# Float16 hi/lo operands for the second layer of a block attention + feed-forward kernel, from the third token group on

## The chip, the cores and the metric

The kernel runs on one core of one Trainium2 chip. The metric is the device time of one execution in microseconds (us); shorter is better. Three runs of the kernel before took 890.31, 891.81 and 893.53 us, median 891.81 us. Engines are named as in the profile: PE is the matrix engine, PEld its weight loads, DVE the vector engine, ACT the scalar engine, POOL the GpSimd engine, SP the engine that issues the DMAs.

## The reference

Attention over independent blocks of 64 positions, for 8 batches and 8 heads of dimension 64, gives 4608 tokens of 512 numbers. A feed-forward part follows, with w_in of 512x2048 and w_out of 2048x512, all in float32:

```python
scores = scale * np.matmul(q_c, k_c.transpose(0, 1, 2, 4, 3))
attn = softmax(scores)
x = np.matmul(attn, v_c)          # 4608 x 512
h = x @ w_in
g = h - np.tanh(h)
return g @ w_out
```

q and k are drawn with a spread of about 0.43, v with 0.1. The result is wanted at close to float32 accuracy, so the kernel splits each operand of a product into a high and a low part and makes three products, hi*hi, hi*lo and lo*hi.

## The kernel before

The 4608 tokens are nine groups of 512 (four tiles of 128). For each group the feed-forward part runs over 16 units; a unit (fc) is a slice of 128 of the 2048 hidden numbers. `FeedForward.gemm1` (L413) makes a unit's hidden slice `ph` in PSUM with 12 matmuls of 512 columns, whose operands are float16 hi/lo pairs (`wih`, `wil`, `xh`, `xl`). `shrink` makes g of it: ACT takes the tanh (L421), DVE makes h - tanh(h) into `t` (L422), ACT rounds it to the high part `gh` (L425), DVE subtracts to get the low part `gl` (L426). Here gh and gl are float32r tiles, and so are the parts `woh`, `wol` of w_out. `gemm2` (L434) then makes 12 matmuls of 512 columns, three (gh*woh, gh*wol, gl*woh) for each of the group's four token tiles, and adds them into four PSUM tiles `po` that gather over all 16 units. gemm2 of a unit is issued two units after its gemm1 (`LAG = 2`), so a group starts with three gemm1 in a row and ends with two gemm2 in a row. `ph`, gh and gl have two buffers each. After the 16 units `finish` copies `po` to SBUF, two tiles by ACT (L459) and two by DVE (L457), and SP writes them out.

Between the units of a group the attention of the next group is worked (`interleaved`), one pair of blocks after another: `split` makes float16 hi/lo parts of q, k, v (ACT L307, L310, L316; DVE L308, L311, L317), `scores` (PE L325), `softmax`, `transpose` by DMA, `values` (PE L359). Since float16 has a narrow range, q, k and v of a group are first multiplied by a power of two. `Late.sums` finds it: `spread` (ACT L96) sums |a| * 2^-12 over 2048 numbers of each partition, once each for q, k and v; POOL takes the maximum over partitions (`power`, L103), and DVE makes the power and its inverse.

The first group is different: in it the weights come in (as bits of 64-bit numbers), are converted, and split; w_in to float16 with a power of its own for each pair of units, w_out to float32r.

What sets the order: the code names, for each half step of a group, what is emitted there (a table `at`; key 2s is after gemm1 of unit s, 2s+1 after the gemm2 that follows). For the first steps PE and SP have an order written out by hand; behind that the framework's scheduler sets each engine's order, and may move an instruction of ACT, DVE or POOL well ahead of where the code names it. On the chip each engine takes its instructions in the order that was built.

## Time and profile before

The profiled execution took 890.42 us, and its span (first to last instruction) is 888.3 us.

| | us |
|---|---|
| median of three runs | 891.81 |
| profiled execution, its span | 890.42, 888.3 |
| first group, until the second starts | 154.25 |
| second group | 91.76 |
| third to eighth group, each | 91.76 |
| ninth group, until its last matmul starts | 85.6 |
| PE busy over the span | 866.5 (98%) |
| DVE busy | 538.5 (61%) |
| ACT busy | 471.3 (53%) |
| POOL busy | 15.5 (2%) |
| mean granted PE clock, share of full | 0.989 |

A line of a group of instructions reads: source line, engine, operation, tile written <- tiles read, shapes, count | busy us in all, mean ns of one | idle us of the engine before them, and what ended that. A line of a timeline reads: start, duration, engine, line, operation, tiles, count, and in brackets the idle time ahead of it and what ended it. Matmuls overlap: one of 512 columns is listed with some 390 ns, and the next starts some 220 ns after it, so the distance of starts is what counts.

### The profile page before, as it was taken

The numbers are of one execution on the slowest core, as the hardware profiler recorded it, in microseconds if no ns is written. First come the engines' busy times: TensorE is split into PE (matmuls) and PEld (weight loads), VectorE is DVE, ScalarE is ACT, GpSimd is POOL, SyncE is SP. The second block draws the span as 40 slices with busy tenths as digits, with TensorE's granted clock in tenths as the row PEclk, the third lists the DMA queues.
The fourth block names the chain that finished last, engine by engine and source line by source line (L and its number), as shares of the span: only waits on it lengthen the run. The fifth ranks groups of instructions, "written<-read, shape, count | busy, mean of one in ns | idle before, by whom it ended". The sixth has DMA issues, their size and how long they took to land.

```text
span 888.3 us, 13109 instructions
## 1 busy us (share of the span) xinstructions
PE 866.5 (98%) x5163; PEld 566.8 (64%) x5163; DVE 538.5 (61%) x976; ACT 471.3 (53%) x824; POOL 15.5 (2%) x32
## 2 busy tenths in 40 slices
PE   7999898999999999999999999999999999999997
PEld 4786655566656666666666666666666666665665
DVE  6798896667666665656466745674567456533222
ACT  8589773756646544555455634663366344423221
POOL 0000003000000000000000000000000000000000
PEclk8899999999999999999999999999999999999999
DMA  9584333312221121212112211132111100010001
GB/s 261 184 233 133 136 122 121 117 36 66 78 83 51 34 72 61 61 47 72 60 53 53 74 60 37 49 89 66 37 48 24 60 13 13 13 54 6 1 1 48
DMA packets 61373, 62.71 MB, mean 71 GB/s; under 512 B 32640, under 2 KB 40832, under 8 KB 61312
## 3 DMA queue, kind: packets, MB, share of 16 engines
q1 hardware_dynamic: 61312, 61.88, 23.8%
q8 instruction: 40, 0.66, 0.3%
q14 instruction: 21, 0.17, 0.1%
HBM read 45.09 MB, written 9.44 MB: 61 GB/s over the span
## 4 chain that ended last, share of the span: by engine, by line
PE 91%; ACT 4%; issue 2%; DVE 2%; DMA 0%; POOL 0%; ACTq 0%; DVEq 0%; POOLq 0%
PE po L434 42%; PE ph L413 40%; PE psa L359 2%; PE psa L325 2%; PE psa L258 2%; PE psa L210 1%; ACT junk L96 1%; ACT s L228 1%; PE ph L501 1%; ACT wih L152 0%; ACT w_out L126 0%; ACT s L241 0%; DVE w_out L127 0%; PE psa L160 0%; ACT w_in L126 0%
## 5 line engine op out<-in xcount | busy, mean ns | idle before, releaser
L434 PE MATMUL po<-woh,gh 128*128 128x512 f32 x576 | 245.6, 426 | 3.3 <-ACT gh L425 3.3
L434 PE MATMUL po<-wol,gh 128*128 128x512 f32 x576 | 225.9, 392 | 0.0
L434 PE MATMUL po<-woh,gl 128*128 128x512 f32 x576 | 225.8, 394 | 0.0
L422 DVE SCALAR_TENSOR_TENSOR t<-ph,sig,t 128x512 f32<-128x512 f32 (+1 forms) x148 | 108.7, 734 | 146.7 <-ACT t L421 146.5
L413 PEld LDWEIGHTS <-wih 128*128 128x128 f16 x1184 | 106.4, 98 | 137.4 <-issue 25.7
L421 ACT ACTIVATE t<-ph,sig 128x512 f32<-128x512 f32 (+1 forms) x148 | 99.8, 674 | 168.0 <-PE ph L413 167.7
L426 DVE TENSOR_TENSOR gl<-t,gh 128x512 fp32r<-128x512 f32 (+1 forms) x148 | 99.8, 675 | 111.4 <-ACT gh L425 111.2
L413 PE MATMUL ph<-xh,wih 128*128 128x512 f16 (+1 forms) x592 | 150.8, 377 | 5.5 <-ACT wih L152 5.5
L425 ACT CAST gh<-t 128x512 fp32r<-128x512 f32 (+1 forms) x148 | 89.4, 604 | 126.0 <-PE po L434 101.5
L413 PE MATMUL ph<-xh,wil 128*128 128x512 f16 (+1 forms) x592 | 149.3, 375 | 0.2 <-DVE wil L153 0.2
L413 PE MATMUL ph<-xl,wih 128*128 128x512 f16 (+1 forms) x592 | 148.5, 373 | 0.0
L434 PEld LDWEIGHTS po<-woh,gh 128*128 128x128 f32 x576 | 108.5, 188 | 34.4 <-ACT gh L425 5.7
L434 PEld LDWEIGHTS po<-woh,gl 128*128 128x128 f32 x576 | 108.0, 188 | 24.5 <-DVE gl L426 0.5
L434 PEld LDWEIGHTS po<-wol,gh 128*128 128x128 f32 x576 | 108.5, 188 | 21.5
L413 PEld LDWEIGHTS <-wil 128*128 128x128 f16 x592 | 58.0, 98 | 67.3 <-issue 1.1
L317 DVE SCALAR_TENSOR_TENSOR v16l<-rawv,to,v16h 64x512 f16<-64x512 f32 x56 | 41.8, 746 | 5.6 <-ACT v16h L316 4.7
L316 ACT ACTIVATE v16h<-rawv,to 64x512 f16<-64x512 f32 x56 | 40.1, 716 | 6.0 <-PE psa L359 4.5
L307 ACT ACTIVATE q16h<-rawq,to 64x512 f16<-64x512 f32 x56 | 40.3, 720 | 4.3 <-DVE exp L297 3.2
L308 DVE SCALAR_TENSOR_TENSOR q16l<-rawq,to,q16h 64x512 f16<-64x512 f32 x56 | 41.6, 744 | 1.3
L345 ACT CAST a<-s 128x512 f16<-128x512 f32 x28 | 17.3, 616 | 30.7 <-DVE s L339 27.9
L333 ACT ACTIVATE s<-s,exp 128x512 f32<-128x512 f32 x28 | 20.1, 719 | 17.2 <-DVE s L332 17.1
L457 DVE COPY t<-po 128x512 f32<-128x512 f32 x18 | 12.4, 690 | 26.8 <-PE po L434 14.3
(98 smaller groups left out, 760.2 us busy)
## 6 DMA issues: line engine op xcount, KB each, us to landing
out<-t SPq DMA_DIRECT2D x36, 256.0 KB, 2.1
raw_in<-w_in SPq DMA_DIRECT2D x16, 512.0 KB, 5.3
raw_out<-w_out SPq DMA_DIRECT2D x16, 512.0 KB, 3.8
rawq<-qL SPq DMA_DIRECT2D x28, 256.0 KB, 2.6
rawk<-kL SPq DMA_DIRECT2D x28, 256.0 KB, 3.0
rawv<-vL SPq DMA_DIRECT2D x28, 256.0 KB, 2.6
qbd<-qE SPq DMA_DIRECT2D x16, 128.0 KB, 4.4
k<-kE SPq DMA_DIRECT2D x8, 256.0 KB, 4.5
```

The costliest lines, as they stand in the source:

```text
L258: nc.tensor.matmul(ps[:, hp, cs], lhsT=d["v"][:, hp, :, c], rhs=d["aT"][:, hp, cs], start=True, stop=True)
L307: nc.scalar.activation(qh[r, :, r], q[r], AF.Copy, scale=to[r, 0:1])
L308: nc.vector.scalar_tensor_tensor(out=ql[r, :, r], in0=q[r], scalar=to[r, 0:1], in1=qh[r, :, r], op0=ALU.mult, op1=ALU.subtract)
L316: nc.scalar.activation(vh[r, :, r], v[r], AF.Copy, scale=to[r, 2:3])
L317: nc.vector.scalar_tensor_tensor(out=vl[r, :, r], in0=v[r], scalar=to[r, 2:3], in1=vh[r, :, r], op0=ALU.mult, op1=ALU.subtract)
L333: nc.scalar.activation(s, s, AF.Exp, scale=d["exp"])
L413: nc.tensor.matmul(ph, lhsT=wi[fc // 2][a][:, fc % 2, kc * P:(kc + 1) * P], rhs=x[b][:, kc, cols], start=(k == 0), stop=(k == 3 * KC - 1))
L421: nc.scalar.activation(t, ph, AF.Tanh, scale=sig)
L422: nc.vector.scalar_tensor_tensor(out=t, in0=ph, scalar=sig, in1=t, op0=ALU.mult, op1=ALU.subtract)
L425: nc.scalar.copy(out=gh, in_=t)
L426: nc.vector.tensor_sub(gl, t, gh)
L434: nc.tensor.matmul(self.po[t], lhsT=gg[a][:, ts], rhs=wo[fc][b], start=(fc == 0 and i == 0), stop=(fc == FC - 1 and i == 2))
```

## The change

From the third group on, gemm2's operands are float16 pairs in place of float32r pairs. Three things make that possible.

* A power of two for w_out (one for all of it), and one for g in each group. That of g comes from a bound: x is a weighted mean of values v, so |x| is at most the largest |v|, and |h| at most that times the sum over a column of |w_in|; `Half.power_of` takes the power of v of this group, a power for w_in and a factor 2^-20. For this bound `Late.sums` now takes v's largest |v| on DVE (`largest`, a TENSOR_REDUCE) where ACT summed |v| before. The inverse is applied when `po` is copied out.
* The maxima of the weights. Over the second group's steps, ACT sums |woh| of each of the 16 units (`spread`, 128x512, and the reading of its sum), DVE takes the largest |wih| of each of 8 pairs of units (128x1024), then `powers` takes the maximum of both over the partitions on POOL (`htop`).
* The conversion, in the second half of the second group. For each unit `convert` adds woh and wol into a float32 tile `whole` on POOL (two buffers), ACT writes the high float16 part and DVE the low one into a new tile of the same name and place as woh (one buffer, so it takes the place of the float32r part once the second group's gemm2 of that unit is done). The second group itself still uses float32r.

In `shrink` ACT's rounding becomes an activation with a scale (gh) and DVE's subtraction a scalar_tensor_tensor (gl), both to float16.

```diff
+    def largest(a, out):
+        nc.vector.tensor_reduce(out=out, in_=a, axis=AX.X, op=ALU.max, apply_absolute_value=True)
+        nc.vector.tensor_scalar_mul(out, out, 2.0 ** -12)
...
             some = self.raw[n][:, :SIZES[g]]
-            spread(self.pool, some, d["sums"][:, "qkv".index(n):"qkv".index(n) + 1])
             if n != "v":
+                spread(self.pool, some, d["sums"][:, "qkv".index(n):"qkv".index(n) + 1])
                 return
+            largest(some.rearrange("p i n -> p (i n)"), d["sums"][:, 2:3])
...
+    class Half:
+        def __init__(self, pool):
...
+        def steps(self):
+            at = defaultdict(list)
+            for fc in range(FC):
+                at[fc + 3].append(lambda fc=fc: spread(self.pool, wo[fc][0].bitcast(F32), self.parts[:, fc:fc + 1]))
+                if fc % 2:
+                    at[fc + 3].append(lambda j=fc // 2: largest(wi[j][0].rearrange("p a n -> p (a n)"), self.w_in[:, j:j + 1]))
+                at[max(FC + 4 + fc, 2 * fc + 2 * LAG + 1)].append(lambda fc=fc: self.convert(fc))
+            at[FC + 3].append(self.powers)
+            return at
+        def powers(self):
+            both = self.pool.tile([P, 2], F32, name="both")
+            nc.vector.tensor_mul(self.w_in, self.w_in, from_w)
+            nc.vector.reduce_max(out=both[:, 0:1], in_=self.w_in, axis=AX.X)
+            nc.vector.reduce_max(out=both[:, 1:2], in_=self.parts, axis=AX.X)
+            power(self.pool, "h", both, self.to, self.back)
+        def convert(self, fc):
+            w = self.pool.tile([P, DM], F32, name="whole", bufs=2)
+            nc.gpsimd.tensor_add(w, wo[fc][0].bitcast(F32), wo[fc][1].bitcast(F32))
+            half = wo_pool[fc].tile([P, DM], F32R, name=f"woh{fc}").bitcast(F16).rearrange("p (a n) -> p a n", a=2)
+            h, l = self.wo[fc] = half[:, 0], half[:, 1]
+            to = self.to[:, 1:2]
+            nc.scalar.activation(h, w, AF.Copy, scale=to)
+            nc.vector.scalar_tensor_tensor(out=l, in0=w, scalar=to, in1=h, op0=ALU.mult, op1=ALU.subtract)
+        def power_of(self, g):
+            to, undo = (const.tile([P, 1], F32, name=n, bufs=2) for n in ("to_g", "undo_g"))
+            nc.vector.scalar_tensor_tensor(out=to, in0=to_x[g], scalar=2.0 ** -20, in1=self.to[:, 0:1], op0=ALU.mult, op1=ALU.mult)
...
@@ shrink
-            gh = ffn.tile([P, MOST], F32R, name="gh")[:, :n]
-            gl = ffn.tile([P, MOST], F32R, name="gl")[:, :n]
-            nc.scalar.copy(out=gh, in_=t)
-            nc.vector.tensor_sub(gl, t, gh)
+            if self.undo_g is not None:
+                gh, gl = (ffn.tile([P, MOST], F32R, name=f"g{a}").bitcast(F16)[:, :n] for a in "hl")
+                nc.scalar.activation(gh, t, AF.Copy, scale=self.to_g)
+                nc.vector.scalar_tensor_tensor(out=gl, in0=t, scalar=self.to_g, in1=gh, op0=ALU.mult, op1=ALU.subtract)
+            else:
...
@@ gemm2
-                    nc.tensor.matmul(self.po[t], lhsT=gg[a][:, ts], rhs=wo[fc][b], start=..., stop=...)
+                    nc.tensor.matmul(self.po[t], lhsT=gg[a][:, ts], rhs=self.wo[fc][b], start=..., stop=...)
...
     for g in range(1, NG):
-        ff = FeedForward(g, x)
+        ff = FeedForward(g, x, half if g > 1 else None)
...
+        at = interleaved(att, g + 1, nx) if nx else {}
+        if g == 1:
+            for k, fs in half.steps().items():
+                at[k] += fs
```

How the built order moves, at three places. The first is ACT from the last unit of the first group to the first units of the second. Before, the two copies of `po` are followed by one sum of |q|, and then the second group's first tanh (`t<-ph,sig`):

```order
L425 CAST gh<-t 128x512
L459 COPY t<-po_104 128x512
L459 COPY t<-po_545 128x512
L96 ACTIVATE junk_1731,sums<-rawq 128x2048
L421 ACTIVATE t<-ph,sig 128x512
L96 ACTIVATE junk_1753,sums<-rawk 128x2048
L425 CAST gh<-t 128x512
L421 ACTIVATE t<-ph,sig 128x512
L96 ACTIVATE junk_1767,sums<-rawv 128x2048
```

Now (`sums_out` are the sums of |woh|):

```order
L490 CAST gh<-t 128x512
L99 ACTIVATE junk_1868,sums_out<-woh_92 128x512
L99 ACTIVATE junk_1909,sums_out<-woh_1091 128x512
L99 ACTIVATE junk_1942,sums_out<-woh_1094 128x512
L99 ACTIVATE junk_1974,sums_out<-woh_1097 128x512
L529 COPY t<-po_104 128x512
L529 COPY t<-po_545 128x512
L99 ACTIVATE junk_1741,sums<-rawq 128x2048
L99 ACTIVATE junk_1999,sums_out<-woh_1100 128x512
L99 ACTIVATE junk_1765,sums<-rawk 128x2048
L481 ACTIVATE t<-ph,sig 128x512 x2
```

Eleven of the 16 sums of |woh| have moved into the first group's tail, the seven before these rows among them, and the first tanh of the second group now stands behind the sum of |q|, a sum of |woh| and the sum of |k|, and the second tanh right behind the first.

The second place is POOL over the second group and later. Before, nothing stands between the fills of the attention's tiles and the maxima of q, k, v of the groups to come (`xtop`):

```order
L279 MEMSET q16l_1629 128x1024
L103 ISA xtop<-sums 128x3 x7
```

Now (an `ISA` row with no tile is a loading of POOL's code for what follows; `htop` is the maximum for the weights):

```order
L287 MEMSET q16l_1629 128x1024
L425 ISA
L425 TENSOR_TENSOR whole<-woh_71,wol_73 128x512
L425 TENSOR_TENSOR whole<-woh_74,wol_75 128x512
L106 ISA
L106 ISA xtop<-sums 128x3
L106 ISA htop<-both 128x2
L425 ISA
...
L425 TENSOR_TENSOR whole<-woh_1103,wol_1105 128x512
L106 ISA
L106 ISA xtop<-sums 128x3
L425 ISA
L425 TENSOR_TENSOR whole<-woh_1106,wol_1107 128x512
L425 TENSOR_TENSOR whole<-woh_1109,wol_1111 128x512
L425 TENSOR_TENSOR whole<-woh_1112,wol_1113 128x512
L106 ISA
L106 ISA xtop<-sums 128x3 x5
```

There are six more loadings, three for the additions and three back for the maxima; the last two before the additions of units 13, 14 and 15 stand around the third group's `xtop`.

The third place is ACT at the end of the second group (`woh<-whole` writes the high part of a converted unit; the last three rows of this kind are units 13, 14, 15):

```order
L490 CAST gh<-t 128x512
L319 ACTIVATE k_2892<-rawk,to 128x512
L429 ACTIVATE woh_2630<-whole,to_half 128x512
L429 ACTIVATE woh_2635<-whole,to_half 128x512
L325 ACTIVATE v16h_1624<-rawv,to 64x8x64
L371 ACTIVATE xh<-psa 128x4x128
L529 COPY t<-po_1645 128x512
L325 ACTIVATE v16h_1624<-rawv,to 64x8x64
L529 COPY t<-po_1647 128x512
L429 ACTIVATE woh_2652<-whole,to_half 128x512
L481 ACTIVATE t<-ph,sig 128x512
```

All three stand ahead of the third group's first tanh (the last row), which so comes after POOL's last addition.

More of the change, by code (lines that the diff above doesn't have):

```diff
@@ L75, in attn_ffn_kernel @@
     wo = [[None, None] for _ in range(FC)]
+    wo_pool = {}
     def weight_tiles(pool, fcs):
@@ L82, in weight_tiles @@
                 wo[fc][i] = pool.tile([P, DM], F32R, name=f"wo{a}{fc}")
+            wo_pool[fc] = pool
     weight_tiles(const, range(EARLY_FC))
@@ L297, in sums @@
             nc.vector.scalar_tensor_tensor(out=d["exp"], in0=d["from"][:, 0:1], scalar=scale, in1=d["from"][:, 1:2], op0=ALU.mult, op1=ALU.mult)
-            from_x[g] = d["from"][:, 2:3]
+            from_x[g], to_x[g] = d["from"][:, 2:3], d["to"][:, 2:3]
         def split(self, g, p, i):
@@ L382, in interleaved @@
         return at
+    class Half:
+        def __init__(self, pool):
+            self.pool = pool
+            self.wo = [None] * FC
+            self.w_in, self.parts = pool.tile([P, FC // 2], F32, name="largest_in"), pool.tile([P, FC], F32, name="sums_out")
+            self.to, self.back = (pool.tile([P, 2], F32, name=n) for n in ("to_half", "from_half"))
+            self.g, self.undo = {}, {}
+        def steps(self):
[24 more added lines that the diff above has]
+            nc.vector.scalar_tensor_tensor(out=to, in0=to_x[g], scalar=2.0 ** -20, in1=self.to[:, 0:1], op0=ALU.mult, op1=ALU.mult)
+            nc.vector.tensor_scalar(out=to, in0=to, scalar1=2.0 ** 100, scalar2=TINY, op0=ALU.min, op1=ALU.max)
+            nc.vector.reciprocal(out=undo, in_=to)
+            nc.vector.tensor_mul(undo, undo, self.back[:, 1:2])
+            return to, undo
@@ L385, in attn_ffn_kernel, with __init__ @@
     class FeedForward:
-        def __init__(self, g, x):
+        def __init__(self, g, x, half=None):
             self.g, self.x, self.queue, self.po = g, x, [], []
+            self.wo, self.undo_g = wo, None
+            if half:
+                self.wo = half.wo
+                self.to_g, self.undo_g = half.power_of(g)
             self.sig, self.known = const.tile([P, FC // 2], F32, name="sig", bufs=2), set()
@@ L433, in gemm2 @@
                 for i, (a, b) in enumerate(((0, 0), (0, 1), (1, 0))):
-                    nc.tensor.matmul(self.po[t], lhsT=gg[a][:, ts], rhs=wo[fc][b], start=(fc == 0 and i == 0), stop=(fc == FC - 1 and i == 2))
+                    nc.tensor.matmul(self.po[t], lhsT=gg[a][:, ts], rhs=self.wo[fc][b], start=(fc == 0 and i == 0), stop=(fc == FC - 1 and i == 2))
         def run(self, units, at, ahead=None):
@@ L455, in finish @@
                 ot = ffn.tile([P, DM], F32, name="t", bufs=3)
-                if t % 2:
+                if self.undo_g is not None:
+                    if t % 2:
+                        nc.vector.tensor_scalar_mul(ot, self.po[t], self.undo_g)
+                    else:
+                        nc.scalar.activation(ot, self.po[t], AF.Copy, scale=self.undo_g)
+                elif t % 2:
                     nc.vector.tensor_copy(ot, self.po[t])
@@ L545, in attn_ffn_kernel @@
     raw_pool.close()
-    att = Late(ctx.enter_context(tc.tile_pool(name="att", bufs=1, side="right", reuse_waits="tile")))
+    late = ctx.enter_context(tc.tile_pool(name="att", bufs=1, side="right", reuse_waits="tile"))
+    att, half = Late(late), Half(late)
     for g in range(1, NG):
         x, nx = nx, new_x() if g + 1 < NG else None
-        ff = FeedForward(g, x)
+        ff = FeedForward(g, x, half if g > 1 else None)
         ff.room(ps_o1, range(2))
         ff.room(ps_o2, range(2, SIZES[g]))
-        ff.run([(fc, 0, SIZES[g]) for fc in range(FC)], interleaved(att, g + 1, nx) if nx else {})
+        at = interleaved(att, g + 1, nx) if nx else {}
+        if g == 1:
+            for k, fs in half.steps().items():
+                at[k] += fs
+        ff.run([(fc, 0, SIZES[g]) for fc in range(FC)], at)
 def kernel(**inputs):
```

6 lines of the change are left out of this document (5 added, 1 removed).

## The prediction

> **What bounds the kernel now.** I read the page's busy shares and its chain of waits first, then the engines by group, then the chain inside one group.
>
> ```profile
> PE 866.5 (98%) x5163; PEld 566.8 (64%) x5163; DVE 538.5 (61%) x976; ACT 471.3 (53%) x824; POOL 15.5 (2%) x32
> PE 91%; ACT 4%; issue 2%; DVE 2%; DMA 0%; POOL 0%; ACTq 0%; DVEq 0%; POOLq 0%
> ```
>
> PE holds 91% of the chain that ended last. By group (columns: window; length; busy us and count of PE, PEld, DVE, ACT, POOL; granted clock; DMA share; GB/s):
>
> ```profile
> 61.00:154.17 93.17, 85.56 (x426) 56.95 (x424) 79.26 (x169) 65.86 (x164) 10.64 (x15) 0.98 0.42 136
> 154.25:246.01 91.76, 91.76 (x578) 59.25 (x577) 62.03 (x109) 59.73 (x89) 0.73 (x2) 1.00 0.27 77
> 246.01:337.77 91.76, 91.76 (x578) 59.22 (x577) 56.18 (x97) 48.39 (x73) 0.37 (x1) 1.00 0.23 62
> 796.57:882.50 85.93, 85.93 (x385) 53.75 (x384) 24.49 (x34) 22.17 (x35) 0.00 (x0) 1.00 0.04 13
> ```
>
> From the second group on PE has no gap at full clock, so a group lasts as long as its matmuls. Most of the first group (first row) loses 93.17 - 85.56 = 7.6 us on PE, with DVE 85% busy. The time can fall only if the matmuls come closer; it rises where ACT, DVE or POOL make PE wait.
>
> **Part 1: gemm2 in float16, groups three to nine.** The start of the fourth group in the chain of waits (start, length), and distances of starts in the ninth group:
>
> ```profile
> 337.93 7.79 PE ph L413 x36
> 345.71 2.77 PE po L434 x12
> 348.48 2.61 PE ph L413 x12
> 351.79 2.81 PE po L434 x12
> 371.47 0.71 PE psa L359 x24
> ...
> 815.57 0.40 PE L434 MATMUL po<-woh,gl 128*128 128x512 f32 x1
> 815.80 0.39 PE L434 MATMUL po<-woh,gh 128*128 128x512 f32 x1
> 816.03 0.39 PE L434 MATMUL po<-wol,gh 128*128 128x512 f32 x1
> 817.87 1.04 PE L413 MATMUL ph<-xh,wih 128*128 128x512 f16 x4
> 818.74 1.03 PE L413 MATMUL ph<-xh,wil 128*128 128x512 f16 x4
> ```
>
> Float32r matmuls of 512 columns start 0.23 us apart, float16 ones (818.74 - 817.87) / 4 = 0.217. A float16 unit of 12 takes 7.79 / 3 = 2.60 us; a gemm2 takes 2.77, or 2.81 where attention scores stand before it (four units of a group). What else than the spacing is in the 2.77 is the change of type ahead of it. Taking gemm1's 2.60 for the new gemm2, a group gains 12 x 0.17 + 4 x 0.21 = 2.9 us. Six groups give 17.4, the ninth, without attention, 16 x 0.17 = 2.7: **20.1 us**. Bounds: nothing, if something else in gemm2 sets the 0.23; about 21 if every gemm2 cost 2.59. I take 20.1, since gemm1 is the same shape with a new weight load each time, in the same stretch.
>
> ```profile
> L434 PEld LDWEIGHTS po<-woh,gh 128*128 128x128 f32 x576 | 108.5, 188 | 34.4 <-ACT gh L425 5.7
> L413 PEld LDWEIGHTS <-wih 128*128 128x128 f16 x1184 | 106.4, 98 | 137.4 <-issue 25.7 <-ACT wih L152 7.8 <-ACT woh L136 0.3
> ```
>
> The added weight-load rows cost nothing: 98 ns lies under 217 of matmul, as in gemm1; uncovered, 1344 of them would cost 132 us. A rule speaks against this term: the Trainium skill ("TensorE: Matmul & The Clock Gate", section on weight-path perf modes) says that the array takes one element per cell per cycle whatever the element's width. By that rule alone the narrower type would gain nothing; 0.23 against 0.217 contradicts it here, and I go by the rows.
>
> gh as a scaled activation and gl as a scalar_tensor_tensor cost some 0.1 and 0.06 us more per unit (0.72 and 0.75 as L152 and L153 below, for 0.62 and 0.69). ACT and DVE work 48 and 56 us of 92 there, so PE covers it; uncovered it is 112 x 0.16 = 18 us. The four small operations of `power_of` stand behind the maxima of the next group, off any chain. v's largest moves 2.1 us per group from ACT to DVE, under PE as well.
>
> **Part 2: the start of the second group.** ACT and DVE before (first group's last units, then the second group):
>
> ```profile
> 146.22 0.69 ACT L421 ACTIVATE t<-ph,sig 128x512 f32<-128x512 f32 x1 [3.59 <-PE ph L413]
> 150.11 0.62 ACT L425 CAST gh<-t 128x512 fp32r<-128x512 f32 x1 [0.82 <-DVE t L422]
> 154.25 1.91 ACT L96 ACTIVATE junk<-rawq 128x2048 bf16<-128x2048 f32 x1
> 156.06 0.19 ACT L96 ACTIVATION_READ_ACCUMULATOR junk<-rawq 128x1 f32 x1
> 157.05 0.69 ACT L421 ACTIVATE t<-ph,sig 128x512 f32<-128x512 f32 x1 [0.80 <-PE ph L413]
> 157.77 0.75 DVE L422 SCALAR_TENSOR_TENSOR t<-ph,sig,t 128x512 f32<-128x512 f32 x1 [1.89 <-ACT t L421]
> 159.44 1.03 PE L413 MATMUL ph<-xh,wih 128*128 128x512 f16 x4
> ...
> L96 ACT ACTIVATE junk<-w_in 128x512 bf16<-128x512 f32 x16 | 10.1, 633 | 0.9 <-DVE w_in L129 0.9
> L96 ACT ACTIVATION_READ_ACCUMULATOR junk<-w_in 128x1 f32 x16 | 3.2, 199 | 0.0
> ```
>
> The group's third gemm1 (159.44) needs the `ph` buffer that DVE frees with the first unit's t (157.77 + 0.75 = 158.5): 0.9 us in hand. A sum of |woh| costs 0.63 + 0.20, about 0.74 in a row, as ACT starts the next instruction some 0.1 early (156.06, not 156.16). From 146.22 ACT now has tanh, two sums, gh, tanh, three sums, gh, four sums and two copies: 4 x 0.58 + 9 x 0.74 + 2 x 0.5 = 10 us, to 156.2. The sum of |q| starts then, 2 us late. Behind it 2.0 + 0.74 + 2.0 us pass until the first tanh at 161, t is done 0.69 + 0.75 later at 162.4, and the third gemm1 starts there in place of 159.44. **Cost 3.0 us**. Bounds: 1.0, if the tail's nine sums all hide (156.2 becomes 154.25), and 4.5, if ACT takes the unoverlapped 0.83 and gh's lateness stops PE at the first group's last gemm2 too.
>
> **Part 3: conversion in the second group.** It adds on ACT five sums and 16 activations of 0.72 and removes a sum of |v|: 59.7 + 4.2 + 11.5 - 2.1 = 73 of 91.8 us. On DVE come 16 residuals of 0.75, two maxima of v (some 2.3 each, bounds 0.7 and 2.7, by 128x512 at 0.68 and four times that), and one of wi: 62.0 + 12 + 4.6 + 1.3 = 80. That is as full as DVE was in the first group; it is hidden by PE as long as only the sum counts, and I put 0.2 us on short waits. The other terms come from these rows:
>
> ```profile
> L152 ACT ACTIVATE wih<-w_in,to_w 128x512 f16<-128x512 f32 x16 | 10.7, 717 | 2.2 <-DVE to_w L109 2.0
> L153 DVE SCALAR_TENSOR_TENSOR wil<-w_in,to_w,wih 128x512 f16<-128x512 f32 x16 | 11.3, 746 | 1.9 <-ACT wih L152 1.9
> L331 DVE TENSOR_REDUCE mx<-psa 128x8 f32<-128x512 f32 x28 | 19.1, 681 | 0.0
> 7.88 0.28 POOL masks.py:199 TENSOR_SCALAR_AFFINE_SELECT ident<-ident 128x128 f32<-128x128 f32 x1 [6.95 <-issue]
> 14.88 0.38 POOL L479 PARTITION_ALL_REDUCE ready<-ready  x1 [6.71 <-DVE w_in L128]
> 145.64 0.95 POOL L279 MEMSET q16l<- 128x1024 f16 x1
> 222.08 0.62 ACT L425 CAST gh<-t 128x512 fp32r<-128x512 f32 x1 [1.85 <-PE po L434]
> 248.86 0.69 ACT L421 ACTIVATE t<-ph,sig 128x512 f32<-128x512 f32 x1 [2.51 <-PE ph L413]
> ```
>
> In both rows with 6.95 and 6.71 us of idle time a code loading stands ahead on POOL: I price one at 6.8. Six are added. The first two, with two additions between them, reach from 146.6 to 162.2, and the maximum behind them needs the sum of |k|, at 161 by part 2; the third and the last have only additions or a distant maximum behind them. The two around the third group's `xtop` are in a chain: addition of unit 12, loading, xtop 0.4, loading, additions 13, 14, 15, then ACT's high part of 15, ahead of the third group's first tanh (248.86 before). Unit 12's addition needs the buffer that the residual of unit 10 frees. In the new order that unit's high part follows the gh at 222.08, so it ends near 223.4, and DVE has gl (0.69) and v's maximum (2.3) at about that place, so the residual ends near 226.5. Addition 12 until 227.5, loadings and maximum until 241.5, additions 13 and 14 until 243.5, 15 behind the residual of 13 until 245, its high part until 245.7: 3 us before the tanh is due. Part 2's delay shifts both alike. An addition of 128x512: no row shows one. Below, half a fill of 1024 (0.5); above, three fills of 1024 (2.85), for two reads and a write; I take 1.0, near the fill. The Trainium skill ("GPSIMD Engine Reference", section on elementwise cycle accounting) gives 4.5 us for an addition of 2048 numbers, so an estimate of 1.1 here; by it the sum stays the same within 0.3 us. Behind ACT's late high parts are queued v's parts, two copies of `po` and the tanh; as ACT and DVE are full just here I put **1.0 us** (bounds 0 and 6, the latter with additions of 2.85 and a loading 1 us longer).
>
> **Sum.** 890.42 - 20.1 + 3.0 + 1.0 + 0.2 = 874.5 us for an execution like the profiled one (span 872.4). The median lies 1.4 above that execution: **876 us**. The last copies of `po` cost the same within 0.2 us.
>
> **Rivals.**
> (A) Preparation hides: ACT's tail has 3.6 us idle at 146.22, and the span falls by the whole 20.1. 871.7 us. Against it stands the order of rows, sums ahead of the tanh.
> (B) POOL comes late: loadings of 9 us in a busy kernel rather than 6.8, or slow additions. Each us beyond the 3 in hand is one on PE at the third group's start: 2 x 2.2 + 3 x 1 - 3 = 4.4 us, 880 us; with additions at the upper bound 882. The loadings before were measured at the start, with DMA at its busiest, which speaks against more.
> (C) The second group queues as the first did: with DVE at 87%, PE loses 7.6 us in place of 1.2. 882 us. For it: the same load. Against it: the first group also waits for weights from DMA.
> (D) The other side: the 0.23 us of gemm2 is not of the type (it could be its three matmuls for one po, then the next), so the spacing stays, and only the costs are left: 891.8 + 4.2 = 896 us, slower. It decides if the spacing falls by less than 4.2 us / 1344 matmuls = 3 ns of the 14. The skill's rule on element width above would end here. Against it: the attention's float16 matmuls also change their place in PSUM every third time, 24 in 0.71 us, with no step.
> (E) The operands don't become float16 on the chip's path, or gains and costs meet by accident: within 0.3%.
>
> **How the numbers follow.** Forecast 0.57, (A) 0.13, (B) 0.12, (C) 0.10, (D) 0.05, (E) 0.03. Time: 876. Range: 871 (A) to 884, with (B) and (C) and a bit of both. A measurement tells 0.3%, 2.7 us: below 889.1 is faster, which forecast, (A), (B), (C) are, 0.92; same 0.03; slower (D) 0.05.
>
> **What would show it.** The third to eighth groups 88.9 us long in place of 91.76, gemm2 2.60 in the chain, matmuls 0.217 apart. A PE gap of about 3 us before the second group's third gemm1, released by DVE's t, with ACT busy ahead. A gap under 2 us at the second group's end or the third's start; POOL idle for 6.8 us ahead of addition 13. It is wrong if gemm2 stays near 2.77, if PE waits inside the second group in many places, or if a group from the fourth on has gaps.

## The result and the profile after

The changed kernel takes 881.58 us (median of six executions, 880.09 to 883.09), the kernel before 891.06 us beside it (six, 887.08 to 893.53). The ratio is 0.9898 with a 95% interval of 0.9872 to 0.9924: 1% faster, 9.5 us. Two more comparisons on other occasions gave 0.9855 (0.9818 to 0.9891) and 0.9875 (0.9838 to 0.9912). The forecast was 876 us.

The busy times of the changed kernel's page, and its chain by engine:

```profile
PE 852.8 (97%) x5162; PEld 459.1 (52%) x5163; DVE 595.5 (68%) x1056; ACT 490.5 (56%) x858; POOL 39.9 (5%) x49
PE 88%; ACT 5%; DVE 3%; DMA 3%; issue 1%; SPq 1%; POOL 0%; ACTq 0%; DVEq 0%; POOLq 0%
```

DVE has 57 us more of work, PE 14 us less. In the chain that ended last PE's share fell from 91% to 88%; DVE has 3% of it (2% before) and DMA 3% (0% before). The third, fourth and ninth group (windows, with the columns of the prediction):

```profile
262.44:351.11 88.67, 88.67 (x578) 43.23 (x578) 61.56 (x103) 48.61 (x71) 0.39 (x1) 1.00 0.22 62
351.11:439.59 88.48, 88.48 (x578) 43.16 (x577) 59.30 (x101) 47.71 (x71) 0.37 (x1) 1.00 0.21 60
793.51:876.50 82.99, 82.99 (x385) 37.49 (x383) 25.55 (x34) 24.04 (x35) 0.00 (x0) 1.00 0.04 14
```

The start of the fourth group in the chain of waits (start, length):

```profile
351.27 7.77 PE ph L473 x36
359.04 2.59 PE po L499 x12
361.63 2.59 PE ph L473 x12
364.22 0.70 PE psa L334 x24
```

A gemm2 takes 2.59 us, exactly as long as a gemm1, and the whole group 88.48 us in place of 91.76. The gain is there, and a little larger than forecast. What took part of it away shows in the groups of PE's instructions (last columns: idle time ahead of them, and who ended it):

```profile
L499 PE MATMUL po<-woh,gl 128*128 128x512 f16 (+1 forms) x576 | 219.8, 385 | 2.4 <-DVE gl L491 2.4
L473 PE MATMUL ph<-xh,wih 128*128 128x512 f16 (+1 forms) x592 | 150.5, 376 | 10.2 <-ACT wih L160 8.1 <-DVE t L482 2.1
```

Before, these two had 0.0 and 5.5 us. Three waits are new or longer: 2.4 us for gl (second group's end), 2.1 us for t (its start), and 5.3 of the 8.1 us for wih (first group's tail; 2.6 before). And each is followed by a stretch in which PE runs slowly. Windows of the changed kernel in the same columns (the last but two is the granted clock), ahead of and behind the three gaps:

```profile
148.00:152.00 4.00, 2.60 (x7) 0.95 (x8) 4.00 (x10) 3.72 (x8) 1.84 (x2) 0.50 0.00 0
152.00:156.00 4.00, 4.00 (x17) 1.64 (x16) 3.09 (x7) 1.51 (x4) 0.00 (x0) 0.81 0.01 4
164.00:168.00 4.00, 3.75 (x18) 1.58 (x17) 4.00 (x6) 4.00 (x6) 0.00 (x0) 1.00 0.51 197
172.00:176.00 4.00, 4.00 (x14) 2.40 (x13) 1.68 (x6) 1.91 (x5) 0.37 (x1) 0.75 0.00 0
260.00:264.00 4.00, 4.00 (x14) 2.30 (x13) 3.97 (x6) 1.80 (x3) 1.03 (x1) 0.65 0.54 197
```

In 4 us at full clock some 18 matmuls of 512 columns start, here 14. The second group's end, in the timeline of PE:

```profile
258.62 0.50 PE L499 MATMUL po<-woh,gl 128*128 128x512 f32 x1 [2.44 <-DVE gl L491]
...
259.45 0.63 PE L499 MATMUL po<-woh,gl 128*128 128x512 f32 x1
259.88 0.63 PE L499 MATMUL po<-woh,gh 128*128 128x512 f32 x1
260.31 0.63 PE L499 MATMUL po<-wol,gh 128*128 128x512 f32 x1
```

They start 0.43 us apart, half speed, for some 3 us. I call what the matmuls behind a gap take beyond 0.2155 us each, summed from their starts, the half clock's cost. With it the two traces compare as follows (losses of PE in us, gap + half clock):

| place | before | after | difference | forecast |
|---|---|---|---|---|
| first gemm1 of the program starts | 34.17 | 39.29 | +5.1 | 0 |
| first group's tail | 2.75 + 1.66 | 5.44 + 2.05 | +3.1 | 0 |
| second group's third gemm1 | 0 | 2.30 + 1.85 | +4.2 | +3.0 |
| second group's end | 0 | 2.60 + 1.79 | +4.4 | +1.0 |
| short waits | | | 0 | +0.2 |
| third to eighth group | 6 x 91.76 | 88.66 + 5 x 88.48 | -19.5 | -17.4 |
| ninth group, to its last matmul | 85.62 | 82.66 | -3.0 | -2.7 |

The sum is -5.7; the last matmul starts 6.0 us earlier (882.18, now 876.17). The first row is not the change's, as the first experiment shows. The span is 7.0 us shorter, since the time from that start to the end of the span fell too, from 6.14 to 5.14 us. This can't be counted for the change either: two kernels made from the one before (one tile more, and fills on DVE, below) took 5.21 and 4.97 us there.

### The profile page after: what moved, and what is told of

Its sections match the earlier page's. It is cut to its first block, busy times and chain, and to the rows that moved or that the text cites. A ratio compares the mean times of both kernels' runs of the same rounds, so it can differ in the third digit from the quotient of the medians.

```text
span 881.3 us, 13271 instructions
## 1 busy us (share of the span) xinstructions
PE 852.8 (97%) x5162; PEld 459.1 (52%) x5163; DVE 595.5 (68%) x1056; ACT 490.5 (56%) x858; POOL 39.9 (5%) x49
## 4 chain that ended last, share of the span: by engine, by line
PE 88%; ACT 5%; DVE 3%; DMA 3%; issue 1%; SPq 1%; POOL 0%; ACTq 0%; DVEq 0%; POOLq 0%
PE ph L473 40%; PE po L499 39%; PE psa L368 2%; PE psa L334 2%; ACT junk L99 2%; PE psa L266 2%; PE psa L218 1%; DMA raw_in<-w_in 1%; DVE w_out L135 1%; DMA rawv<-vL 1%; ACT s L236 1%; DMA rawk<-kL 1%; ACT wih L160 0%; DMA vbd<-vE 0%; ACT t L481 0%
## 5 line engine op out<-in xcount | busy, mean ns | idle before, releaser
L499 PE MATMUL po<-woh,gh 128*128 128x512 f16 (+1 forms) x1024 | 321.4, 385 | 3.3 <-ACT gh L490 3.3
L499 PE MATMUL po<-woh,gl 128*128 128x512 f16 (+1 forms) x576 | 219.8, 385 | 2.4 <-DVE gl L491 2.4
L473 PEld LDWEIGHTS <-wih 128*128 128x128 f16 x1184 | 113.1, 99 | 141.7 <-ACT wih L160 10.4
L486 DVE SCALAR_TENSOR_TENSOR gl<-t,to_g,gh 128x512 f16<-128x512 f32 x112 | 84.0, 750 | 90.5 <-ACT gh L485 89.6
L499 PEld LDWEIGHTS <-gh 128*128 128x128 f16 x896 | 85.6, 98 | 98.7
L485 ACT ACTIVATE gh<-t,to_g 128x512 f16<-128x512 f32 x112 | 80.6, 719 | 89.4 <-PE po L499 75.2
L499 PEld LDWEIGHTS <-gl 128*128 128x128 f16 x448 | 43.8, 98 | 52.9
L499 PE MATMUL po<-wol,gh 128*128 128x512 f32 x128 | 51.1, 399 | 0.0
L499 PEld LDWEIGHTS po<-woh,gh 128*128 128x128 f32 x128 | 24.5, 191 | 11.5 <-ACT gh L490 5.5
L499 PEld LDWEIGHTS po<-woh,gl 128*128 128x128 f32 x128 | 24.3, 190 | 8.6 <-DVE gl L491 3.1
```

The lines of the kernel that those rows point to most:

```text
L473: nc.tensor.matmul(ph, lhsT=wi[fc // 2][a][:, fc % 2, kc * P:(kc + 1) * P], rhs=x[b][:, kc, cols], start=(k == 0), stop=(k == 3 * KC - 1))
L485: nc.scalar.activation(gh, t, AF.Copy, scale=self.to_g)
L486: nc.vector.scalar_tensor_tensor(out=gl, in0=t, scalar=self.to_g, in1=gh, op0=ALU.mult, op1=ALU.subtract)
L499: nc.tensor.matmul(self.po[t], lhsT=gg[a][:, ts], rhs=self.wo[fc][b], start=(fc == 0 and i == 0), stop=(fc == FC - 1 and i == 2))
```

## The experiments

All runs, with the kernel before in the same comparison; the last column is where the first gemm1 starts in the profile.

| kernel | median us | before | ratio (95%) | first gemm1 |
|---|---|---|---|---|
| the change again | 880.59 | 893.75 | 0.9855 (0.9818 to 0.9891) | 39.31 |
| no search | 875.53 | 893.75 | 0.9805 (0.9773 to 0.9837) | 36.44 |
| no additions | 874.83 | 893.75 | 0.9801 (0.9772 to 0.9829) | 37.76 |
| idle additions | 883.84 | 893.75 | 0.9886 (0.9847 to 0.9924) | 39.90 |
| before, one tile more | 895.34, one run | 894.70 | | 37.51 |
| fills on DVE | 878.50 | 894.70 | 0.9823 (0.9799 to 0.9846) | 37.76 |
| before, fills on DVE | 889.01 | 894.70 | 0.9938 (0.9915 to 0.9962) | 35.95 |
| spread | 870.27 | 894.70 | 0.9740 (0.9713 to 0.9767) | 34.27 |
| before again | 895.95, one run | 893.19 | | 39.09 |
| additions on DVE | 878.07 | 893.19 | 0.9835 (0.9805 to 0.9864) | 37.51 |
| the change, third time | 882.33 | 893.19 | 0.9875 (0.9838 to 0.9912) | 40.07 |

**The same two kernels again.** No edit.

> The changed kernel as it is, a second time. In its first trace the first group's matmuls of gemm1 start at 51.78 us instead of 46.65 (PE runs at a granted clock of .6 and at half its busy share around 20 to 30 us), and in the tail of the first group one TENSOR_SCALAR of w_out on VectorE takes 5.52 us beside six back-to-back POOL MEMSETs (2.84 us beside three in the kernel before). Theory 'chance of the run': the order of every engine is the same up to there, so gemm1 starts near 46.7 to 48 in this trace, and the span is some 4 to 5 us below 881.3, about 876 to 878. Rival 'the change does it': gemm1 starts at 51 to 52 again and the span is 880 to 882. On the TENSOR_SCALAR: if the ports of VectorE and GpSimd collide, it again lasts about as long as the row of MEMSETs that it falls into, whatever their number.

> The kernel before as it is, for a second profile of its start. In ten profiles so far (three of programs made from the kernel before, seven from the changed one, all with the same instructions in the same order up to there) the first gemm1 starts between 34.2 and 39.9 us, early where the first 32 matmuls of the scores run 0.118 us apart and late where they run 0.213 apart. Theory 'chance of the run': the start of this profile need not be that of the first one (34.17); anything between 34 and 40 us, and the span differs from 888.3 by as much. Rival 'the kernel sets it': 34.2 again within 0.3 us and the span 888.3 within 1 us.

> The changed kernel a third time, beside the same runs of the kernel before as the one with additions on VectorE. By all theories 880 to 883 us; its start shows once more whether 39.3 us, seen twice, is fixed by the kernel (39.3 again) or a chance of the run (34 to 40).

The first repeat spoke for the rival: gemm1 at 39.31 us again, the span 881.3 again. The other two settled it. The second profile of the kernel before has its first gemm1 at 39.09 us, not 34.17, and a span of 893.9 in place of 888.3. The scores at the start (timeline of PE) in the first profile of the kernel before:

```profile
5.21 4.23 PE L210 MATMUL psa<-k,qbd 128*128 128x64 f32 x32
```

In its second profile:

```profile
5.34 7.06 PE L210 MATMUL psa<-k,qbd 128*128 128x64 f32 x32
```

And in the first profile of the changed kernel:

```profile
5.55 7.06 PE L218 MATMUL psa<-k,qbd 128*128 128x64 f32 x32 [0.35 <-DMA k<-kE]
```

The same 32 matmuls took 4.23 or 7.06 us in the same kernel. Over all thirteen profiles, whose orders are the same up to there, the first gemm1 started between 34.17 and 40.07 us (the expectation of the first repeat names a later matmul, at 46.65 and 51.78). So the start is a chance of the run, worth up to 6 us, and the first profile of the kernel before had caught the earliest. Between two profiles with alike starts (39.09 and 39.29) the span falls from 893.9 to 881.3, 12.6 us, of which 1.0 lies behind the start of the last matmul (6.16 and 5.14 us). The Trainium skill ("TensorE: Matmul & The Clock Gate", part 1, on what is happening) says that the clock is set by a free-running window of activity, so that the same kernel has more or fewer slow matmuls at its start from run to run; the traces agree. In the kernel without additions, below, the distance of these matmuls goes from 0.118 to 0.214 us at 8.3 us, where the granted clock goes from 1.00 to 0.50.

The long TENSOR_SCALAR came back unchanged (5.52 us), so that is no chance.

**The search left out** (`no_search`): `powers` and the steps of `steps` that feed it.

```diff
-                at[fc + 3].append(lambda fc=fc: spread(self.pool, wo[fc][0]...))
-                    at[fc + 3].append(lambda j=fc // 2: largest(wi[j][0]...))
@@ powers
-            power(self.pool, "h", both, self.to, self.back)
+            for i, e in enumerate((15, 9)):
+                nc.vector.memset(self.to[:, i:i + 1], 2.0 ** e)
+                nc.vector.memset(self.back[:, i:i + 1], 2.0 ** -e)
```

> Leaves out the search for the largest weights in the second group (no sums of |woh| on ACT, no maxima of wih on DVE, no maximum over partitions for them); two fixed powers, 2^15 and 2^9, stand in their place. Theory 'ACT's row' (part 2 of the prediction): the sums ahead of the first tanh made PE wait before the second group's third gemm1, so the gap of 2.2 us there and the 1.5 us behind it go, the first tanh comes within 1.5 us of the group's start plus 3 as in the kernel before, and the time is 3.5 to 4 us below the changed kernel's, about 878. Rival 'raw data late': the sum of |q| itself comes late for another reason (the tail of the first group), so a gap of over 1.5 us stays there and the time falls by less than 1.5 us. The end of the second group (gap of 2.4 us) stays as it is by both.

875.53 us, 5.1 below the changed kernel beside it. PE's waits from 150 to 262 us in it:

```profile
PE po L492 <- DVE gl L484: 2.6, 2, 2.1
```

The wait for t at the second group's start is gone, with the half clock behind it; of gl's two waits one is 0.43 us, the other that of the group's end, 2.1. So the search makes that gap. Whether ACT's sums alone do, as part 2 has it, is not shown, since the maxima of wih on DVE are left out in the same run. In the changed kernel (timeline of ACT and DVE):

```profile
167.71 1.21 DVE L116 TENSOR_REDUCE largest_in<-wih 128x1 f32<-128x1024 f16 x1
168.38 1.26 ACT L481 ACTIVATE t<-ph,sig 128x512 f32<-128x512 f32 x2
169.09 1.41 DVE L482 SCALAR_TENSOR_TENSOR t<-ph,sig,t 128x512 f32<-128x512 f32 x2 [0.18 <-ACT t L481]
```

DVE, busy without a break since 159.5 us, was done with its maxima and copies at 168.92, 0.18 us before the tanh was there. In this order an earlier tanh alone would have brought t forward by no more than that.

The two spans (874.8 and 881.3) differ by 6.5 us: 4.2 for this place, 2.9 for the chance of the start and 0.9 for a shorter gap in the first group's tail, less 0.5 for a longer half clock behind that, 0.6 for the short wait for gl and 0.4 in the third group.

**No additions, and additions for nobody** (the last two lines of the diff are in the second kernel only). Both leave wol out of the float16 pair, which is made from woh alone and put in wol's place.

```diff
-            w = self.pool.tile([P, DM], F32, name="whole", bufs=2)
-            nc.gpsimd.tensor_add(w, wo[fc][0].bitcast(F32), wo[fc][1].bitcast(F32))
-            half = wo_pool[fc].tile([P, DM], F32R, name=f"woh{fc}")...
+            w = wo[fc][0].bitcast(F32)
+            half = wo_pool[fc].tile([P, DM], F32R, name=f"wol{fc}")...
...
+            junk = self.pool.tile([P, DM], F32, name="whole", bufs=2)
+            nc.gpsimd.tensor_add(junk, w, h)
```

> Leaves out the additions of woh and wol on GpSimd: high and low part are made from woh alone and written into wol's place, so POOL has no additions and no loadings around them; ACT and DVE do exactly as many high and low parts as before. Theory 'POOL': the gap of 2.4 us at the second group's end (PE waiting for DVE's gl) goes to under 0.5 us, and the time is 2 to 3 us below the changed kernel's, about 879. Rival 'ACT and DVE are full': the 16 high and 16 low parts alone make the queue, so a gap of 1.5 us or more stays near the second group's end and the time falls by less than 1 us. The gap before the second group's third gemm1 stays by both.

> As the kernel without additions (high and low part made from woh alone, into wol's place), but GpSimd still adds 16 times 128x512 float32, woh and the high part, into a tile that nobody reads: nobody waits for POOL any more, and POOL works as much as in the changed kernel. Theory 'port': while POOL adds, DVE operations that read two operands from SBUF stretch (q16l took 1.76 us instead of 0.75, gl 1.05 instead of 0.69), so the same stretching is seen, a gap of 1.5 us or more at the second group's end can come back, and the time is above the kernel without additions by 1 to 3 us. Rival 'chain': only the wait for POOL's results mattered, so the time is that of the kernel without additions within 0.7 us and the gap is under 0.5 us.

874.83 us without additions, 883.84 with the idle ones, 880.59 with the change's. Without them the time fell by 5.8 us, more than the 2 to 3 expected. The traces (881.3 and 872.7, 8.6 us) say where: 4.2 for the gap at the group's end and the half clock behind it, 1.6 since the gap at the group's start was not followed by half clock this time, 1.2 in the first group's tail (a shorter row of fills, see below) and 1.6 for the chance of the start. Only the 4.2 is what was tested. PE's waits from 150 to 265 us without additions:

```profile
PE ph L472 <- DVE t L481: 2.2, 1, 2.2
```

With idle additions:

```profile
PE po L500 <- DVE gl L492: 3.2, 1, 3.2
PE ph L474 <- DVE t L483: 2.2, 1, 2.2
```

The gap at the group's end needs the additions, but nobody has to wait for their result: it comes from POOL and DVE working at one time. In the changed kernel itself (timeline of DVE and POOL):

```profile
254.32 3.52 DVE L317 SCALAR_TENSOR_TENSOR q16l<-rawq,to,q16h 64x512 f16<-64x512 f32 x2
254.35 2.95 POOL L425 TENSOR_TENSOR whole<-woh,wol 128x512 f32<-128x512 f32 x2 [7.13 <-DVE v16l L326]
257.88 0.69 DVE L491 TENSOR_TENSOR gl<-t,gh 128x512 fp32r<-128x512 f32 x1
```

Two q16l, 0.75 us each elsewhere, take 3.52 us beside two additions in a row, 2.0 us too long, and gl, for which PE waits 2.44 us, stands behind them. With idle additions (timeline of DVE) it is two q16l, k (0.75 us elsewhere) and gl itself (0.69 elsewhere), together 2.6 us too long for a wait of 3.2:

```profile
254.28 2.36 DVE L317 SCALAR_TENSOR_TENSOR q16l<-rawq,to,q16h 64x512 f16<-64x512 f32 x2
256.68 1.53 DVE L320 SCALAR_TENSOR_TENSOR k<-rawk,to,k 128x512 f16<-128x512 f32 x1
258.13 1.63 DVE L492 TENSOR_TENSOR gl<-t,gh 128x512 fp32r<-128x512 f32 x1
```

The second group as a window, without additions and with idle ones:

```profile
154.20:254.02 99.82, 97.65 (x601) 63.59 (x601) 86.50 (x158) 75.19 (x128) 1.10 (x3) 1.00 0.23 67
157.20:263.69 106.49, 101.10 (x602) 65.01 (x600) 93.30 (x159) 75.33 (x128) 21.97 (x18) 0.97 0.23 65
```

DVE was busy for 86.5 and 93.3 us, with one instruction of difference (158 and 159): some 6.8 us of stretching for 16 additions. The Trainium skill ("GPSIMD Engine Reference", key points) states that GpSimd shares its ports to SBUF with VectorE and that the two contend when VectorE has two inputs from SBUF; the rows agree. The prediction had not weighed it.

One chain over POOL stays even with idle additions: the third group's maximum (`xtop`), before which DVE can't start on that group's q, k and v, stands behind additions and loadings. It ran at 246.83 us in the changed kernel, at 244.90 with idle additions and at 236.01 without. It can't have made much of the gap: from 236.6 us to the late gl of the changed kernel DVE stood idle for more than 0.1 us only once, for 0.79 us, and then for ACT.

**The additions on DVE** (`add_dve`).

```diff
-            nc.gpsimd.tensor_add(w, wo[fc][0].bitcast(F32), wo[fc][1].bitcast(F32))
+            nc.vector.tensor_add(w, wo[fc][0].bitcast(F32), wo[fc][1].bitcast(F32))
```

> The changed kernel with one edit: the additions of woh and wol on VectorE in place of GpSimd (16 times 0.69 us more on VectorE in the second group, no addition and no loading on GpSimd, the result the same). Theory 'port': the operations of VectorE that stretched beside the additions cost more than the additions themselves would, so the gap of 2.6 us at the second group's end goes to under 1.2 us, the half clock behind it too, and the time is 2.5 to 6 us below the changed kernel, 875 to 878. Rival 'VectorE is full': 11 us more of work make it queue, a gap over 1.5 us or several of 1 us stay, and the time is within 1.5 us of the changed kernel's.

878.07 us beside 882.33 of the changed kernel: 4.3 less. The additions cost DVE 10.9 us in all, and PE had no wait for gl (groups of instructions):

```profile
L425 DVE TENSOR_TENSOR whole<-woh,wol 128x512 f32<-128x512 f32 x16 | 10.9, 687 | 0.1
L499 PE MATMUL po<-woh,gl 128*128 128x512 f16 (+1 forms) x576 | 219.0, 384 | 0.0
```

So DVE, with 11 us of work more, is better off than beside POOL's additions. (The maximum `xtop` comes earlier here too, at 239.63 us.)

**One tile more in the kernel before** (`before_tile`).

```diff
-    att = Late(ctx.enter_context(tc.tile_pool(name="att", ...)))
+    late = ctx.enter_context(tc.tile_pool(name="att", ...))
+    att = Late(late)
+    nc.vector.memset(late.tile([P, 1320], F32, name="unused"), 0.0)
```

> The kernel before with one tile more in the pool of the later attention (5280 bytes in each partition, as much as the change's new tiles take there), written once by VectorE and never read; nothing else is changed. Theory 'place': the tile moves the zero-filled tiles to addresses that are free earlier, so GpSimd's MEMSETs run in a longer row (six in place of three), the TENSOR_SCALAR of w_out that falls into it takes about 5.5 us in place of 2.84, and PE's step before the last units' wih is 5.7 us in place of 2.98. Rival 'order': the change's own instructions made the longer stall, so the row is three MEMSETs and the step is 3.0 as before. On the start of the program: the first scores run at a spacing of 0.118 or of 0.213 us by chance; at 0.118 the first gemm1 starts at 34 to 36 us, at 0.213 at 39 to 40.

One execution, 895.34 us, is too little to tell a difference in time; what counts is its trace. The tail in the timeline of the kernel before, with the first and the last of three fills in a row, the fourth, and DVE's operation:

```profile
136.27 1.02 POOL L279 MEMSET v16h<- 128x1024 f16 x1
136.51 2.84 DVE L127 TENSOR_SCALAR w_out<-w_out 128x512 uint32<-128x512 uint32 x1
138.05 1.02 POOL L279 MEMSET v16h<- 128x1024 f16 x1
142.04 0.95 POOL L279 MEMSET v16l<- 128x1024 f16 x1 [2.97 <-DVE w_out L129]
```

With the tile, the first and the last of six in a row, and the seventh:

```profile
139.62 1.02 POOL L279 MEMSET v16h<- 128x1024 f16 x1
139.85 5.52 DVE L127 TENSOR_SCALAR w_out<-w_out 128x512 uint32<-128x512 uint32 x1
144.08 1.02 POOL L279 MEMSET q16l<- 128x1024 f16 x1
148.07 0.95 POOL L279 MEMSET q16h<- 128x1024 f16 x1 [2.97 <-DVE w_out L129]
```

An unused tile alone makes the longer stall. By the rows not the fourth fill but the seventh is now the first that waits for DVE's last work on w_out. That the tile does this by moving the filled ones to other addresses, and that a fill may run as soon as the memory of its tile is free, is how I read it; no view shows addresses. DVE's operation, 0.42 us elsewhere, ends some 0.3 us behind the row. All kernels with the fills on POOL lie on one line:

| fills in a row | DVE's operation | PE's gap | where |
|---|---|---|---|
| 3 | 2.84 | 2.75 | kernel before |
| 4 | 3.73 | 3.65 | no additions |
| 5 | 4.63 | 4.56 | no search |
| 6 | 5.52 | 5.44 | changed kernel; before with one tile more |

The Trainium skill ("Advanced Engine Details and Errata", VectorE performance modes) says that GpSimd's instructions and VectorE's in a mode that uses both ports block each other; here one instruction waited out the whole row, not one fill. That it was in such a mode is argued from its speed, 0.42 us for 512 columns where DVE's operations with two inputs take 0.69 to 0.75.

**The fills on DVE**, in the changed kernel and in the one before.

```diff
-            for t in self.v16[0] + self.v16[1] + self.q16[0] + self.q16[1]:
-                nc.gpsimd.memset(t, 0.0)
@@ the loop over groups
+            for i, t in enumerate(att.v16[0] + att.v16[1] + att.q16[0] + att.q16[1]):   # g == 1
+                at[i // 2].append(lambda t=t: nc.vector.memset(t, 0.0))
```

> The changed kernel with the eight zero fills of the attention's tiles on VectorE, at the start of the second group, in place of GpSimd in the first group's tail. Theory 'lock-out': the TENSOR_SCALAR of w_out takes 0.4 us, PE's gap of 5.4 us before the last units' wih shrinks to under 1 us, and the half clock behind it (2.05 us lost) goes too: 6 to 7.5 us less than the changed kernel, about 874. Rival 'the weights come late': the gap is that of the maximum for the last weights (wtop) or of their load, so 3 us or more of it stay and the time falls by less than 2.5 us. The two gaps of the second group stay by both.

> The kernel before with the same edit: the eight zero fills on VectorE at the start of the second group. Theory 'lock-out': the gap of 2.75 us goes to under 1 us and the half clock behind it (1.66 us lost) too, so the time is 3.5 to 4.5 us below the kernel before. Rival 'the weights come late': gap and time stay within 1.5 us. Between this kernel and the changed one with the same fills stands the change without the stall that it lengthened: by the groups' gain of 22.4 us and the two gaps of the second group with the half clock behind them (4.2 and 4.4 us), 13.8 us.

The kernel before falls by 5.7 us, somewhat more than expected. The changed one falls to 878.5 only, by the ratios of its three comparisons 0.3 to 0.8% below the changed kernel (3 to 7 us), and by the traces 4.4 us, 1.5 of it the chance of the start, in place of the 6 to 7.5 expected. The stall itself went as expected (DVE's timeline):

```profile
140.18 0.42 DVE L135 TENSOR_SCALAR w_out<-w_out 128x512 uint32<-128x512 uint32 x1
```

But PE's waits from 150 to 262 us are these:

```profile
PE po L497 <- ACT gh L488: 3.5, 2, 2.0
PE po L497 <- DVE gl L489: 2.4, 1, 2.4
PE psa L366 <- DMA aT<-a: 1.8, 1, 1.8
PE ph L471 <- DVE t L480: 1.4, 1, 1.4
```

Three are new, two for gh and one for a transposed tile. Against the changed kernel's trace the tail is some 7 us shorter (5.1 of gap, and the 2.05 of half clock behind it), and the second group gives 3.8 us back. DVE's rows there show a and gl at 1.76 to 1.78 us beside POOL's additions again; that the additions make these new waits too is argued from that, no run shows it alone. Between the two kernels with the same fills the change is worth 10.5 us, less than the 13.8 expected, by about what these waits cost.

**All of it together** (`spread`): fills on DVE, additions on DVE, half of the sums of |woh|, |k|'s sum and |v|'s maximum tied to the first units of the second group, ten of the sixteen units converted in the third group.

```diff
+            self.small: 2^-12, made on DVE from gh of the second group's third unit
-  at[fc + 3]: spread(self.pool, wo[fc][0], self.parts[:, fc:fc + 1])
+  at[PIN + 1 + fc if fc >= 8 else fc]: spread(..., self.small if fc >= 8 else 2.0 ** -12)
-  at[max(FC + 4 + fc, 2 * fc + 2 * LAG + 1)]: self.convert(fc)
+  second group: at[PIN + FC + 3 + fc * 3 // 2]: self.convert(fc) for fc < 6
+  third group:  at[max(6, 2 * fc - 6)]: self.convert(fc) for fc >= 6
@@ convert
+            nc.vector.scalar_tensor_tensor(out=w, in0=woh, scalar=self.one, in1=wol, op0=ALU.mult, op1=ALU.add)
```

> The changed kernel with the zero fills on VectorE and its preparation spread: half of the sums of |woh|, the sum of |k| and the maximum of |v| are tied to a value that is there only after the second group's first units, the additions of woh and wol are on VectorE, six units are converted in the second group and ten in the third, each before its gemm2 there. Theory 'queue and port': both gaps of the second group (2.3 and 2.6 us) and the half clock behind them (1.85 and 1.79 us) go, at the price of short waits of 1 to 3 us around the third group's start: 5 to 7 us below the kernel with the fills alone, about 868. Rival 'VectorE is full': with 11 us of additions more VectorE sets the pace in the second and third group, the third is longer than 90.5 us, and the time is that of the kernel with the fills alone or above.

870.27 us (five executions, 867.41 to 873.49), 8.2 us below the kernel with the fills alone in the same comparison (5 to 7 were expected) and the best of this study: it beats both kernels. The second, third and fourth group (windows):

```profile
145.20:245.20 100.00, 98.32 (x602) 63.71 (x601) 94.90 (x178) 73.07 (x123) 1.80 (x3) 1.00 0.24 69
245.20:335.05 89.85, 88.63 (x576) 43.16 (x576) 65.19 (x112) 51.98 (x77) 0.37 (x1) 1.00 0.22 62
335.05:423.53 88.48, 88.48 (x577) 43.15 (x576) 59.40 (x101) 47.82 (x71) 0.37 (x1) 1.00 0.21 60
```

The clock is 1.00 throughout (0.97 in the changed kernel's second group), the waits around the third group's start are 0.3, 0.7, 0.7 and 1.2 us, and none of them is followed by half clock. DVE at 95 of 100 us did not set the pace.

## Why the prediction was right, and where not

The direction, the place of the gain and the range held; the forecast was 5.6 us too low. That the range held owes something to luck: the costs came to 11.7 us in place of 4.2, and 2.4 us more of gain made up for a part; without that the time would have been 884.0, the range's upper end. Step by step:

**Part 1** was right in kind and 2.4 us too small: -22.5 in place of -20.1. A group gained 3.28 us, not 2.9. The gemm2 takes 2.59 us where I had put 2.60, and gemm1 itself and the attention's pieces became a hundredth or so shorter each (7.77 for 7.79, 0.70 for 0.71), 16 and 8 times a group. Rival (D) is refuted. The rule on element width of the Trainium skill ("TensorE: Matmul & The Clock Gate", weight-path perf modes) does not give the spacing for this pair of types: 0.216 us (2.59 / 12) between the starts of float16 matmuls against 0.23 in float32r. Whether the array itself or the longer weight load (188 ns against 98) sets the 0.23, no run separates.

**Part 2**, 3.0 us: the place and the releaser were right, and leaving out the search took the gap away. The term was 1.2 us too small. Its gap was 2.3 us; the half clock behind it, 1.85 us, was not in the sum. And it followed ACT alone: DVE's row of maxima and copies ended only 0.18 us earlier and would have held t nearly as long.

**Part 3** is where the prediction failed, in its step "as ACT and DVE are full just here I put 1.0 us", and in the sentence ahead of it that the work "is hidden by PE as long as only the sum counts". The term measured 4.4 us: 2.6 us of gap and 1.8 of half clock. The chain over POOL that I worked out was near the truth (loadings of 6 to 7.5 us, additions 1.28 us alone where I took 1.0, as these rows of POOL's timeline show), and it was not the main cause: the idle additions, for which nobody waits, make the same gap. The cause is that POOL's additions stretch DVE's operations, 2.0 us right ahead of the late gl. I had costed each engine alone, and none of the rows that I quoted had POOL and DVE at work on SBUF at one time; the one that did, DVE's 2.84 us beside three fills in the tail, was in the trace and I passed over it. DVE's sum for the second group, 80 us, was short as well: six maxima of wih fell into it (7.2 us) where I counted one (1.3), and the stretching came on top: 92.9 us. Without additions it measured 86.5, and there was no gap at the group's end.

```profile
158.63 2.53 POOL L425 TENSOR_TENSOR whole<-woh,wol 128x512 f32<-128x512 f32 x2 [6.90 <-DVE t L482]
168.62 0.39 POOL L106 PARTITION_ALL_REDUCE xtop<-sums  x1 [7.45 <-ACT junk L99]
...
206.82 1.28 POOL L425 TENSOR_TENSOR whole<-woh,wol 128x512 f32<-128x512 f32 x1 [1.71 <-DVE woh L430]
```

**Not foreseen at all**: the first group's tail, +3.1 us. The change adds tiles to a pool, and with them the fills run in a longer row. No order of instructions shows that.

**The rivals.** (C) named 882 us and the second group, and its time was met, but not its way: PE loses there in two gaps with a named releaser each, one of them POOL's doing, and 3.6 us of it in half clock. (B), POOL late, named 880 us; but PE waits for gl at the second group's end and not for POOL's results at the third's start, and the idle additions make the same gap. (A) falls with the gap before the third gemm1. (E) falls with the groups' length.

**What the base was worth.** I made the sum against one profiled execution, with 1.4 us to the median. Its start was an early one, 5 us below the kernel's second profile, so the sum stood on a base that flattered the kernel before. As a difference the forecast was 15.8 us; the three comparisons measured 9.5, 13.2 and 10.9.

**When the clock falls.** Of six gaps of 2.3 us at the second group's start five were followed by half clock, and the sixth, in the kernel without additions, was not. The traces' records of the granted clock tell why. In all thirteen profiles the clock changes only at times that are a whole number of 3.41 us apart (in the changed kernel at 146.73, 153.56, 170.62, 174.04, 259.37 and 262.79 us). What counted was how much of one such stretch PE stood idle:

| profile | stretch | PE idle in it | clock in the next |
|---|---|---|---|
| no additions | 165.31 to 168.72 | 1.96 | 1.00 |
| no search | 249.91 to 253.32 | 2.13 | 0.50 |
| changed kernel | 167.21 to 170.62 | 2.15 | 0.50 |
| changed kernel | 255.96 to 259.37 | 2.44 | 0.50 |

From 60 us to the last matmul every stretch at full clock with 2.13 us of idle PE or more was followed by half clock, and none with 1.96 or less, in all thirteen profiles. In the kernel without additions the gap (165.10 to 167.27) was as long as in the others, but the border at 165.31 cut it. So whether a gap of 2 to 3 us costs only itself is a chance of where it falls.

## What to carry to other kernels

Cost an instruction that is moved to POOL on DVE as well: here 16 additions on POOL cost DVE 6.8 us by stretching its operations, against the 10.9 us that they cost when DVE did them itself, and they did it in front of what PE was waiting for. A PE gap above some 2 us cost nearly twice its length in most cases here, because of the half clock behind it; several gaps of about 1 us cost only themselves, so it pays to break a long wait into short ones. Look where new tiles come to lie: 5 KB in a pool made a stall of 2.7 us longer by 2.7 us without a single instruction on the path being moved.

## What the runs showed of the hardware that was not expected

* Half clock already behind 2.13 us of idle PE within one stretch of 3.41 us, and never behind 1.96 or less (granted clock 0.75 and 0.65 in the 4 us behind the two gaps of the second group, matmuls 0.43 us apart for about 3 us, 1.6 to 1.9 us lost there). The Trainium skill ("TensorE: Matmul & The Clock Gate", why this matters) sets the bound for idle gaps at about 3 us; in these runs it was lower.
* One VectorE instruction of 0.42 us, with one tile as input, waited out a row of 3 to 6 GpSimd fills to the end: 2.84, 3.73, 4.63, 5.52 us, 0.89 more per fill. Operations with two inputs from SBUF took up to 1.8 us in place of 0.69 to 0.75 beside GpSimd additions.
* GpSimd stood idle for 6.0 to 7.5 us at three of the four changes between additions and maxima over partitions in the changed kernel (7.45 and 7.13 in the rows above, 5.99 before the `xtop` at 246.83; at the fourth it waited longer, for ACT), and for 6.90 between the fills and the first addition; between a maximum (135.88 + 0.52) and a fill (136.27) it did not.
* The first 40 us of the program differ by up to 5.9 us between profiles with the same instructions in the same order, with the speed of PE's first scores.
